# A new order of the first four blocks, other due times for later work, and 48 weight columns in the state sums of the second head

## The chip, the cores and the metric

The kernel runs on one core of a Trainium2 chip. Its engines work side by side, each in its own program order: TensorE (PE in the profile, with its weight loads apart as PEld), VectorE (DVE), ScalarE (ACT), GpSimd (POOL) and SyncE (SP). All transfers between DRAM and the core's memory are issued on SyncE's queue. The metric is the device time of one execution in microseconds (us), as the median of several runs; three runs of the kernel before gave 516.4 to 516.85 us, median 516.7 us.

## The reference

Attention with a decaying state, and behind it a feed-forward layer with a squared relu. B = 4 sequences, H = 8 heads, S = 768 steps, D = 48; 3072 tokens, 384 model columns, 2048 hidden columns.

```python
for t in range(S):
    state = alpha[:, :, t, :, None] * state + np.einsum('bhd,bhe->bhde', k[:, :, t], v[:, :, t])
    y[:, :, t] = np.einsum('bhd,bhde->bhe', q[:, :, t], state)
...
x = np.ascontiguousarray(attn_out.transpose(0, 2, 1, 3)).reshape(B * S, H * D)
h = np.maximum(x @ w_in, 0.0)
return (h * h @ w_out).astype(np.float32)
```

`w_in` and `w_out` arrive as 64-bit floats, which the kernel turns into 32-bit ones itself.

## The kernel before

**Blocks.** A block is 128 steps of one sequence, all heads: 24 blocks, numbered so that blocks 0 to 3 are the first 128 steps of the four sequences, 4 to 7 the next, and so on. Attention goes by blocks, two (a pair) at a time. The steps of a block n each have a short name, which the lists of the program use:

- `load`: q, k, v or alpha (a) of the block, 192 KB each, on SyncE's queue (L122)
- `ln`: logarithm of alpha (ACT, L267); `cs`: its running sum by a matmul with a triangle of ones (PE, L288, L291, L292)
- `eb`, `ei`: exp of the sums, and of their negative (ACT, L302, L305, L310)
- `mq`, `mk`: q and k scaled with these (DVE, L314)
- `qT`, `kT` and `qc`, `kc`: scaled q, k turned by four PE transposes each (L355) and copied out of PSUM (L371). From block 4 on `turn` does all of a pair's 32 transposes (T, L529) and ACT copies (L537)
- `sc`: scores inside each half of the block (PE, L418, bank `sckv`); `kv`: the block's contribution to the state, a sum over the steps of each half (PE, L441, the other part of that bank); `am`: masked scores (DVE, L426); `us`, `st`: state in the middle and at the end of the block (DVE, L452; L466, L467, the last one with the factors `last`)
- the last row of exp of the sums has to become a column, `last`. The first four blocks transpose it on PE (`lt`, L343) and copy it (`lc`, L349); later ones write it to DRAM (`bl`, L327) and read it back turned (`br`, L333, `last<-row`)
- `ya`, `yb`: the pair's output y (PE, L398), with a GpSimd nop between the two parts; `ga` and `gb` are the same with the scores, sums and state of the next pair ahead of them. `ea`, `ed`, `ev`: y copied into the transposed input x of the feed-forward (ACT and DVE, L562)

PSUM has eight banks, one pool (tag `att`) for everything.

**Feed-forward.** Four blocks, 512 tokens, make a group; there are six. Group 0 goes in plain f32: `ffn_in` (L926) computes a 128-column stripe j of the hidden layer, three matmuls, `ha` and `hb` are its two halves of 256 tokens, which a pair each makes ready; the output side (L760) follows. From group 1 on, weights and x are each split into a coarse part, a rest and a difference, and each product goes in three passes of a faster type (`h`, L681; `o`, L843, L855, L760). The parts of the weights are made on ACT and DVE by `prepare` (`cast_w`, `rest_w`, `diff_w`), those that don't fit are written to DRAM (`keep`) and streamed back for each group by `pump` (L644), as long as the number of tiles held is under `room`; the pool has 26 buffers.

**Weights.** Eight pieces of `w_in` and eight of `w_out`, 768 KB each. A piece is converted from 64 bits in three steps: `first` (DVE, two passes, L174 and L178), `middle` (ACT, L187 and L190), `second` (DVE, three passes, L196, L200, L203).

**What sets the order.** The first four blocks, the first three weight pieces and the first halves of group 0 stand in a list that is written out by hand (`first`, L980 to L989): each word calls a step, and every engine gets its instructions in the order of the words. `zeros2` there is three matmuls of a zero state tile with 256 columns (L384), `warm` one such (L244): fillers without a result. The words `gt`, `gs`, `gk`, `gy` hold the next load until an instruction of PE is done. Behind the list, `weave` (L1052) walks the units of the feed-forward, each with a cost, and puts in events (attention steps, weight conversions, splits) whose due time is reached. A pair's steps are due at the offsets of `PLAN` (L996) behind the pair's start, `EARLY` (L1011) for blocks under 8; the starts (`g0`, `g1`, `g`), the offsets of `ga` and `gb`, the spacing of the copies of y (`evs`), the start of the splits of x (`g1x`, `gx`), the pieces' preparation (`w_first`, `wstep`, `w_in_at`, `w_in_by`, `o0`, `o2`), the number of splits of the hidden layer put ahead (`lead`, `s0`, `ahead`) and `room` stand in the table `AT` (L19), all in units.

The state sums use 64 of k's columns as weights for both heads of a pair of heads: the first head writes partitions 0 to 63, the second 64 to 127 of the bank, of which 48 each are needed (the 16 between are zeros):

```python
out=ps[h][64 * e : 64 * (e + 1), 1, p, G:64],
lhsT=tile_of("k", n)[HALF[h], 2 * p + e, :],
```

Of the kernel before, what the change touches and what calls it, by code (L numbers as in the profile page):

```python
# [9 lines left out]
FP32 = mybir.dt.float32  # L10
# [5 lines left out]


GB = 4
AT = {'u0': 2, 'evs': 0.4, 'lead': 4, 'post': 3, 'w_first': (45.82, 44.44, 94.99), 'wstep': 2.31, 'w_in_at': 1.92, 'w_in_by': 3.02, 'room1': 25, 'room': 26, 's0': 3, 'ahead': 12, 'late': 23, 'xs': 0.35, 'g0': (-0.17, 20.59, 27.02), 'sc0': (2.36, 2.26, 2.42), 'g1': (7.68, 18.74, 27.21), 'g': (2.3, 15.42), 'g1x': 47.42, 'gx': 39.86, 'g0x': 55.51, 'k0': 2, 'h0': 16, 'k1': 5, 'h1': 0, 'h1by': 5, 'evs0': 0.23, 'tp': 'DDAD', 'tp1': 'AADD', 'split': 8, 'o0': (42.39, 46.35), 'o1': (), 'o2': (21.54, 19.65, 30.49, 26.1, 43.38, 50.96), 'str1': 14.0, 'ga': 9.32, 'gb': 12.97}  # L19


RUN = {0: 128, 32: 32, 64: 64, 96: 32}
# [3 lines left out]
def kernel(  # L26
# [12 lines left out]
    nc = tc.nc  # L39
    B, H, S, D = q.shape  # L40
    C = 128
    NCH = S // C
    NP = H // 2
# [4 lines left out]
    G = 64 - D  # L48
# [7 lines left out]
    ps_att = ctx.enter_context(tc.tile_pool(name="ps_att", bufs=8, space=PSUM))  # L56
# [11 lines left out]
    s_t = [s_all.pop(0) for _ in range(B)]  # L68
# [30 lines left out]
    def tile_of(x, n):  # L99
        return lent.get((x, n), tiles[x][n % len(tiles[x])])  # L100
# [142 lines left out]
    def warm(_):  # L243
        nc.tensor.matmul(  # L244
            out=ps_att.tile([128, NP, 64], FP32, tag="att", name="warm"),
            lhsT=s_t[0].rearrange("a p d -> a (p d)")[:, 0:128], rhs=s_t[0], start=True, stop=True,
        )

    for _ in range(3):
        warm(0)  # L250


    blk = [{} for _ in range(NBLK)]
# [16 lines left out]

    SPLIT = AT["split"]

# [135 lines left out]
    HALF = [slice(0, 64), slice(64, C)]  # L408
# [26 lines left out]
    def state_sums(n):  # L435
        ps = two[n]
        for p in range(NP):
            for e in range(2):
                first = (2 * p + e) * D
                for h in range(1 if n // B == NCH - 1 else 2):  # L440
                    marks["k", n] = nc.tensor.matmul(  # L441
                        out=ps[h][64 * e : 64 * (e + 1), 1, p, G:64],
                        lhsT=tile_of("k", n)[HALF[h], 2 * p + e, :],
                        rhs=tiles["v"][n % NV][HALF[h], first : first + D],
                        start=True, stop=True, skip_group_check=True,
                    )

    def sums_copied(n):

        ps = two.pop(n)  # L450
        u = blk[n]["u"] = u_all[n % 3]
        nc.vector.tensor_tensor(  # L452
            out=own(u), in0=own(ps[0][:, 1]), in1=own(s_t[n % B]), op=ALU.add
        )
        blk[n]["kv1"] = own(ps[1][:, 1])

    def own(x):
        return x[:, :, G:64]

    def next_state(n):  # L460
        blk[n]["s"] = s_t[n % B]
        if n // B < NCH - 1:
            s_all.append(s_t[n % B])
            s_t[n % B] = s_all.pop(0)
            s, last = own(s_t[n % B]), last_t[n % 4].unsqueeze(2).to_broadcast([128, NP, D])
            nc.vector.tensor_tensor(out=s, in0=blk[n].pop("kv1"), in1=own(blk[n]["u"]), op=ALU.add)  # L466
            nc.vector.tensor_tensor(out=s, in0=s, in1=last, op=ALU.mult)  # L467

# [118 lines left out]
    here, todo, room = {}, [], [22]  # L587
# [37 lines left out]
    def diff_w(w, p):  # L625
# [95 lines left out]
    def splits_of_x(at, g):  # L721
        return [(at + i * AT["xs"], f, (g, i % KM)) for i, f in enumerate((split_x,) * KM + (diff_x,) * KM)]

    def layer_in(g):
        units = []
        for n in range(NJ + 2):
            if n < NJ:
                units.append((1.05, in_x, (n,)))
            if 0 <= n - 2 < NJ:
                units.append((0.53, in_y, (n - 2,)))  # L730
            if 0 <= n - AT["post"] < NJ:
                units.append((0, in_post, (n - AT["post"],)))
            if AT["lead"] <= n < AT["lead"] + AHEAD and (g > 1 or AT["k1"] == NW):
# [240 lines left out]
    for x in "stky":  # L974
# [3 lines left out]
    steps["hb"] = lambda j: ffn_in(0, j, slice(HT, 2 * HT))  # L978
    steps["first"], steps["middle"], steps["second"] = convert_first, convert_middle, convert_second
    first = """  # L980
        zeros2 ln0 cs0 ln1 eb0 cs1 load0v ei0 mq0 mk0 load2a eb1 qT0 load3a qc0 mq1
        kT0 kc0 load1v ei1 qT1 mk1 load2k load2q qc1 sc0 kT1 weights0 kc1 kv0 load3q
        am0 lt1 sc1 ln2 us0 ln3 cs2 lt0 am1 load3k kv1 cs3 eb2 us1 ei2 gt1 mk2
        load2v weights1 ya0 mq2 yb0 lc1 gy0 eb3 kT2 lc0 load3v qT2 ei3 load4a zeros2
        st0 ea00 kc2 qc2 ed01 ed02 first0 zeros2 load4q mq3 zeros2 mk3 qT3 middle0
        qc3 kT3 second0 first1 kc3 lt3 lt2 sc2 kv2 am2 ea03 us2 sc3 kv3 gk3 middle1
        weights2 lc3 am3 us3 ha0 ya2 yb2 second1 weights3 ea20 lc2 ed21 ha1 ha3
        weights4 ed22 ed23 first2 st2 middle2 ha2 hb0 load4v hb1 st3 st1 load4k
    """  # L989
    for word in first.split():  # L990
        f = max((x for x in steps if word.startswith(x)), key=len)
# [2 lines left out]


    PLAN = (  # L996
        (-1.2, "ln0 ln1"),
        (-0.5, "sp0"),
        (0.0, "sp1"),
        (2.5, "cs0 cs1 eb0 ei0"),  # L1000
        (3.0, "eb1 ei1"),
        (3.5, "mk0"),
        (4.0, "bl0"),
        (4.5, "mq0 mk1 bl1"),
        (5.0, "mq1"),
        (6.5, "turn br1"),
        (7.0, "kc0 qc0 kc1 qc1 br0"),
        (9.5, "ga"),
        (10.5, "gb"),
    )  # L1010
    EARLY = (  # L1011
# [91 lines left out]
    for g in range(1, NG):  # L1103
        events = []
        if g + 1 < NG:
            n = GB * (g + 1) + 2
# [4 lines left out]
        if g == 1:  # L1111
# [5 lines left out]
            n = min(AT["k0"], AT["k1"])  # L1117
# [41 lines left out]
```

## Time and profile before

| | us |
|---|---|
| median of 3 runs | 516.7 |
| profiled execution, span from the first to the last instruction | 514.6 |
| TensorE busy | 508.3 |
| VectorE busy | 377.0 |
| ScalarE busy | 302.3 |
| GpSimd busy | 6.0 |

The page of the profile gives busy times by engine, and a line of the span in 40 slices, each digit the busy share (or the granted TensorE clock, PEclk) in tenths. The chain of waits is followed back from the last instruction; its pieces carry a start, a duration and the work. Rows of the timeline have a start, a duration, engine, line, operation, output and input with shapes, a count, and in brackets the idle time before and what ended it. Rows of grouped instructions have count, busy time, mean in ns, and idle time with its releaser. Rows of the stretches carry the busy time of each engine with its count of instructions, then the granted clock, the share of the DMA engines and GB/s. Rows of the waits: who waited for whom, the sum, how often, the longest. A matmul in f32 leaves two records.

The span begins with loads (the first logarithm starts at 3.68 us, the second at 6.90 us); blocks 0 and 1 have their y at 16 to 18 us, blocks 2 and 3 at 28 to 30 us; group 0's input side runs to 76.9 us, its output side to 124.5 us, group 1 to 212.3 us, and the last matmul ends at 511 us.

### The profile page before, as it was taken

What the parts mean: (1) busy time and instruction counts of PE and PEld (TensorE: products, weight loads), DVE (VectorE), ACT (ScalarE), POOL (GpSimd) and SP (SyncE); (2) the same over time, 40 slices, a digit from 0 to 9 for tenths busy, and PEclk for the clock granted to TensorE, in tenths of its full rate; (3) what the DMA queues carried; (4) which work ended last, traced back from release to release, by engine and by line L of the source; (5) the groups of instructions that cost most, each with busy time, mean ns of one, the idle gap of its engine ahead of it and who ended that gap; (6) DMA issues with size and microseconds to landing.
All of it is one profiled execution on the core that took longest, in us unless ns stands there. A gap on an engine that the chain in (4) does not pass through costs nothing.

```text
span 514.6 us, 12773 instructions
## 1 busy us (share of the span) xinstructions
PE 508.3 (99%) x5166; PEld 404.6 (79%) x5166; DVE 377.0 (73%) x656; ACT 302.3 (59%) x627; POOL 6.0 (1%) x33
## 2 busy tenths in 40 slices
PE   8999999999999999999999999999999999999997
PEld 6884456669877679988888888888888888888996
DVE  3798899898789869886698286799275588274961
ACT  4789875677788576376764175855075663144520
POOL 4000000000000000000000000000000000000000
PEclk9999999999999999999999999999999999999999
DMA  9989867272797788799975678894775544789201
GB/s 171 226 238 269 233 177 226 33 224 101 267 238 199 189 188 234 263 330 222 241 187 154 209 220 229 222 225 146 227 221 168 186 128 151 214 277 401 88 0 63
DMA packets 144794, 102.73 MB, mean 200 GB/s; under 512 B 116560, under 2 KB 118240, under 8 KB 144736
## 3 DMA queue, kind: packets, MB, share of 16 engines
q1 hardware_dynamic: 144736, 101.92, 70.4%
q8 instruction: 41, 0.67, 0.6%
q14 instruction: 17, 0.14, 0.1%
HBM read 84.57 MB, written 17.33 MB: 198 GB/s over the span
## 4 chain that ended last, share of the span: by engine, by line
PE 96%; DMA 2%; SPq 1%; DVE 1%; issue 0%; ACT 0%; DVEq 0%; POOLq 0%
PE h L681 31%; PE o L760 22%; PE o L843 13%; PE h L931 8%; PE o L855 6%; PE y L398 4%; PE sckv L418 3%; PE T L529 2%; PE sckv L441 2%; PE cs L288 1%; DMA a_in<-in_alpha_dram 1%; PE zeros L384 1%; DMA last<-row 1%; PE cs L291 1%; SPq L333 1%; PE cs L292 1%
## 5 line engine op out<-in xcount | busy, mean ns | idle before, releaser
L696 ACT ACTIVATE hid<-h 128x512 f32<-128x512 f32 x56 | 33.7, 601 | 88.4 <-PE h L681 86.7
L681 PE MATMUL h<-xd,wd 128*128 128x512 f32 x240 | 68.4, 398 | 0.0
L681 PE MATMUL h<-xa,wb 128*128 128x512 f32 x240 | 67.8, 391 | 0.0
L681 PE MATMUL h<-xl,wl 128*128 128x512 f32 x240 | 67.6, 390 | 0.0
L594 DVE TENSOR_TENSOR hid<-h,hid 128x512 f32<-128x512 f32 x56 | 38.5, 689 | 33.9 <-PE h L681 33.6
L562 ACT COPY x<-y 32x256 f32<-32x256 f32 (+1 forms) x137 | 48.9, 365 | 8.7 <-PE y L398 6.4
L681 PEld LDWEIGHTS h<-xl,wl 128*128 128x128 f32 x240 | 45.0, 188 | 9.6
L681 PEld LDWEIGHTS h<-xa,wb 128*128 128x128 f32 x240 | 44.9, 188 | 9.4
L681 PEld LDWEIGHTS h<-xd,wd 128*128 128x128 f32 x240 | 43.7, 188 | 9.2
L760 PE MATMUL o<-w_out,hid 128*128 128x384 f32 x144 | 48.9, 492 | 0.0
L931 PE MATMUL h<-x,w_in 128*128 128x512 f32 (+1 forms) x120 | 43.0, 511 | 0.0
L655 ACT ACTIVATE ha<-hid 128x512 fp32r<-128x512 f32 x42 | 26.7, 638 | 26.1 <-DVE hx L656 12.8
L760 PEld LDWEIGHTS o<-w_out,hid 128*128 128x128 f32 x144 | 26.7, 190 | 17.2
L710 DVE SCALAR_TENSOR_TENSOR hid<-hid 128x512 f32<-128x512 f32 x56 | 37.8, 684 | 0.0
L931 PEld LDWEIGHTS h<-x,w_in 128*128 128x128 f32 x120 | 22.4, 190 | 16.9 <-issue 13.9
L855 PE MATMUL o<-hd,wd 128*128 128x512 f32 x144 | 33.4, 391 | 0.0
L656 DVE SCALAR_TENSOR_TENSOR hl<-ha,hid 128x512 fp32r<-128x512 f32 x42 | 28.8, 686 | 4.7 <-ACT ha L655 4.4
L855 PEld LDWEIGHTS o<-hd,wd 128*128 128x128 f32 x144 | 26.8, 188 | 6.1 <-ACT o L848 0.6
L594 DVE TENSOR_TENSOR hd<-ha,hl 128x512 fp32r<-128x512 f32 x42 | 29.1, 692 | 1.9
L843 PE MATMUL o<-hx,wb 128*128 128x512 f32 x72 | 28.4, 394 | 0.0
L843 PE MATMUL o<-hx,wl 128*128 128x512 f32 x72 | 28.0, 389 | 0.0
L843 PE MATMUL o<-ha,wb 128*128 128x512 f32 x72 | 28.0, 389 | 0.0
(130 smaller groups left out, 950.4 us busy)
## 6 DMA issues: line engine op xcount, KB each, us to landing
wd<-do SPq DMA_DIRECT2D x37, 384.0 KB
wl<-lo SPq DMA_DIRECT2D x34, 384.0 KB
wl<-li SPq DMA_DIRECT2D x32, 384.0 KB
wd<-di SPq DMA_DIRECT2D x32, 384.0 KB
raw<-in_moe_w_in_dram SPq DMA_DIRECT2D x8, 768.0 KB
raw<-in_moe_w_out_dram SPq DMA_DIRECT2D x8, 768.0 KB
v_in<-in_v_dram SPq DMA_DIRECT2D x24, 192.0 KB
a_in<-in_alpha_dram SPq DMA_DIRECT2D x22, 192.0 KB
```

Source lines behind the costliest of these rows:

```text
L398: ins = nc.tensor.matmul(out=ys[e][64 * half : 64 * half + D + G * e, m % 2, p // 2, t], lhsT=lhsT, rhs=rhs, start=(half, e) not in seen, ...
L562: copy(out=x[kk][to : to + m, t : t + 2], in_=blk[n]["y"][e][r : r + m, :, p // 2],)
L594: nc.vector.tensor_tensor(out=o, in0=x, in1=z, op=op)
L655: nc.scalar.activation(out=a, in_=x, func=AF.Copy, scale=NEAR * E)
L656: nc.vector.scalar_tensor_tensor(out=l, in0=a.bitcast(FP32), scalar=-1.0 / E, in1=x, op0=ALU.mult, op1=ALU.add)
L681: nc.tensor.matmul(out=acc["h", j], lhsT=here[w, "i", p][:, kk, jj * 128 : (jj + 1) * 128], rhs=x_parts[x][:, kk], start=start and kk == 0 ...
L696: nc.scalar.activation(out=hid[j], in_=x, func=AF.Copy, scale=E)
L710: nc.vector.scalar_tensor_tensor(out=h, in0=h, scalar=0.0, in1=h, op0=ALU.max, op1=ALU.mult)
L760: nc.tensor.matmul(out=acc[t][:, 0:DM], lhsT=lhs[:, t * C : (t + 1) * C], rhs=rhs, start=start, stop=stop, skip_group_check=True,)
L843: nc.tensor.matmul(out=acc[c], lhsT=by_parts(here[w, "o", p], jj, c), rhs=x, start=n == 0 and w == "b", stop=n == NJ - 1 and w == "l", ski ...
L855: nc.tensor.matmul(out=acc[c], lhsT=by_parts(here["d", "o", p], n % 2, c), rhs=h_diff[n], start=False, stop=last and n == NJ - 1, skip_gro ...
L931: nc.tensor.matmul(out=ps, lhsT=w[:, kk, c0 : c0 + 128], rhs=xT[g][kk][:, cols], start=(kk == 0), stop=(kk == KM - 1),)
```

## The change

The list of the first four blocks is reordered. The first weight load goes ahead of v of block 1, `first0` ahead of the first masks, `middle0` ahead of the scaling of k of block 2; the fillers become seven `warm` (three ahead of the list as before) and three `zeros2` (before: three and four); the weight pieces, the copies of y and the half stripes `ha`, `hb` change places. `PLAN` and `AT` get other numbers, among them `g` from (2.3, 15.42) to (2.59, 16.44), `ga` from 9.32 to 9.22, `gb` from 12.97 to 13.41, `g1` from (7.68, 18.74, 27.21) to (9.3, 18.13, 28.01), `g1x` from 47.42 to 51.0, `gx` from 39.86 to 41.05, `lead` from 4 to 5, `s0` from 3 to 4, `ahead` from 12 to 10, `room1` (group 1) from 25 to 23, `room` from 26 to 27, `str1` from 14.0 to 2.65, `w_first` from (45.82, 44.44, 94.99) to (40.13, 41.4, 99.74), `o0` from (42.39, 46.35) to (41.66, 48.39). A new tile `pad` is taken from the PSUM pool behind the first three fillers, with no matmul in it (`pad` is 0). The second head's state sums take 48 weight columns, write partitions 64 to 111, and the VectorE steps on the state cover 112 partitions.

```diff
+    ps = ps_att.tile([128, NP, 64], FP32, tag="att", name="pad")
+    for _ in range(AT["pad"]):
+        nc.tensor.matmul(
...
-                first = (2 * p + e) * D
+                first, wide = (2 * p + e) * D, D if e else 64
...
-                        out=ps[h][64 * e : 64 * (e + 1), 1, p, G:64],
-                        lhsT=tile_of("k", n)[HALF[h], 2 * p + e, :],
+                        out=ps[h][64 * e : 64 * e + wide, 1, p, G:64],
+                        lhsT=tile_of("k", n)[HALF[h], 2 * p + e, 0:wide],
...
     def own(x):
-        return x[:, :, G:64]
+        return x[0 : 64 + D, :, G:64]
...
     first = """
-        zeros2 ln0 cs0 ln1 eb0 cs1 load0v ei0 mq0 mk0 load2a eb1 qT0 load3a qc0 mq1
-        kT0 kc0 load1v ei1 qT1 mk1 load2k load2q qc1 sc0 kT1 weights0 kc1 kv0 load3q
-        am0 lt1 sc1 ln2 us0 ln3 cs2 lt0 am1 load3k kv1 cs3 eb2 us1 ei2 gt1 mk2
-        load2v weights1 ya0 mq2 yb0 lc1 gy0 eb3 kT2 lc0 load3v qT2 ei3 load4a zeros2
-        st0 ea00 kc2 qc2 ed01 ed02 first0 zeros2 load4q mq3 zeros2 mk3 qT3 middle0
-        qc3 kT3 second0 first1 kc3 lt3 lt2 sc2 kv2 am2 ea03 us2 sc3 kv3 gk3 middle1
-        weights2 lc3 am3 us3 ha0 ya2 yb2 second1 weights3 ea20 lc2 ed21 ha1 ha3
-        weights4 ed22 ed23 first2 st2 middle2 ha2 hb0 load4v hb1 st3 st1 load4k
+        zeros2 warm0 ln0 cs0 ln1 load0v cs1 eb0 load2a eb1 ei0 mq0 mk0 lt1 qT0 mq1 kT0 ei1
+        kc0 qT1 warm0 ln2 cs2 mk1 load3a kT1 weights0 qc0 load1v qc1 first0 kc1 eb2 sc0 ln3
+        kv0 ei2 load2k lt0 sc1 kv1 warm0 am0 warm0 cs3 load2q load3q us0 load3k weights1
+        lc0 load2v am1 us1 middle0 mk2 eb3 ya0 yb0 load3v kT2 gy0 lc1 mq2 mq3 qT2 ei3 ea00
+        st0 gt1 zeros2 mk3 qT3 qc2 zeros2 ed02 kT3 ed01 kc2 qc3 first1 load4q load4a kc3
+        lt3 sc2 kv2 sc3 lt2 kv3 ea03 second0 am2 middle1 am3 ha0 us2 us3 lc2 ya2 load4k yb2
+        lc3 gk3 weights3 ea20 second1 ed22 ed21 first2 weights4 ha1 weights2 load4v ed23
+        middle2 ha3 ha2 st1 st2 hb1 st3 hb0
     """
...
     PLAN = (
-        (-1.2, "ln0 ln1"),
-        (-0.5, "sp0"),
-        (0.0, "sp1"),
-        (2.5, "cs0 cs1 eb0 ei0"),
-        (3.0, "eb1 ei1"),
-        (3.5, "mk0"),
-        (4.0, "bl0"),
-        (4.5, "mq0 mk1 bl1"),
-        (5.0, "mq1"),
-        (6.5, "turn br1"),
+        (-0.93, "ln0 ln1"),
+        (-0.63, "sp0"),
+        (-0.51, "sp1"),
+        (2.25, "cs0 cs1 eb0 ei0"),
+        (2.73, "eb1 ei1"),
+        (3.14, "mk0"),
+        (4.49, "bl0"),
+        (4.57, "mq0 mk1 bl1"),
+        (5.02, "mq1"),
+        (6.99, "turn br1"),
         (7.0, "kc0 qc0 kc1 qc1 br0"),
-        (9.5, "ga"),
+        (9.64, "ga"),
         (10.5, "gb"),
     )
```

More of the change, by code (lines that the diff above doesn't have):

```diff
@@ L18 @@
 GB = 4
-AT = {'u0': 2, 'evs': 0.4, 'lead': 4, 'post': 3, 'w_first': (45.82, 44.44, 94.99), 'wstep': 2.31, 'w_in_at': 1.92, 'w_in_by': 3.02, 'room1': 25, 'room': 26, 's0': 3, 'ahead': 12, 'late': 23, 'xs': 0.35, 'g0': (-0.17, 20.59, 27.02), 'sc0': (2.36, 2.26, 2.42), 'g1': (7.68, 18.74, 27.21), 'g': (2.3, 15.42), 'g1x': 47.42, 'gx': 39.86, 'g0x': 55.51, 'k0': 2, 'h0': 16, 'k1': 5, 'h1': 0, 'h1by': 5, 'evs0': 0.23, 'tp': 'DDAD', 'tp1': 'AADD', 'split': 8, 'o0': (42.39, 46.35), 'o1': (), 'o2': (21.54, 19.65, 30.49, 26.1, 43.38, 50.96), 'str1': 14.0, 'ga': 9.32, 'gb': 12.97}
+AT = {'pad': 0, 'u0': 2, 'evs': 0.21, 'lead': 5, 'post': 3, 'w_first': (40.13, 41.4, 99.74), 'wstep': 2.47, 'w_in_at': 2.02, 'w_in_by': 2.52, 'room1': 23, 'room': 27, 's0': 4, 'ahead': 10, 'late': 23, 'xs': 0.26, 'g0': (-0.17, 20.59, 27.17), 'sc0': (2.3, 2.23, 2.45), 'g1': (9.3, 18.13, 28.01), 'g': (2.59, 16.44), 'g1x': 51.0, 'gx': 41.05, 'g0x': 55.56, 'k0': 2, 'h0': 18, 'k1': 5, 'h1': 0, 'h1by': 5, 'evs0': 0.42, 'tp': 'DDAD', 'tp1': 'AADD', 'split': 8, 'o0': (41.66, 48.39), 'o1': (), 'o2': (21.47, 19.65, 32.98, 28.08, 41.44, 51.99), 'str1': 2.65, 'ga': 9.22, 'gb': 13.41}
 RUN = {0: 128, 32: 32, 64: 64, 96: 32}
@@ L250 @@
         warm(0)
+    ps = ps_att.tile([128, NP, 64], FP32, tag="att", name="pad")
+    for _ in range(AT["pad"]):
+        nc.tensor.matmul(
+            out=ps[:, 0, 0:8], lhsT=s_t[0].rearrange("a p d -> a (p d)")[:, 0:128],
+            rhs=s_t[0][:, 0, 0:8], start=True, stop=True,
+        )
     blk = [{} for _ in range(NBLK)]
@@ L464, in next_state @@
             s_t[n % B] = s_all.pop(0)
-            s, last = own(s_t[n % B]), last_t[n % 4].unsqueeze(2).to_broadcast([128, NP, D])
+            s, last = own(s_t[n % B]), last_t[n % 4][0 : 64 + D].unsqueeze(2).to_broadcast([64 + D, NP, D])
             nc.vector.tensor_tensor(out=s, in0=blk[n].pop("kv1"), in1=own(blk[n]["u"]), op=ALU.add)
```

## The prediction

> **What bounds the kernel now.** I read the page's busy times first, then TensorE's own waits, then the chain of work that ended last, piece by piece, and only then the first 30 us engine by engine.
>
> ```profile
> span 514.6 us, 12773 instructions
> PE 508.3 (99%) x5166; PEld 404.6 (79%) x5166; DVE 377.0 (73%) x656; ACT 302.3 (59%) x627; POOL 6.0 (1%) x33
> PEclk9999999999999999999999999999999999999999
> ```
>
> TensorE is busy in all but 6.3 us, at the granted clock throughout, so apart from its own work only gaps and fillers can move the time. Behind the first 2 us its matmuls show two waits of 0.2 us or more for another engine's result (a third, for a copy of k, is as short as the second):
>
> ```profile
> PE cs L288 <- ACT a_in L267: 0.5, 1, 0.5
> PE sckv L418 <- DVE hid L594: 0.2, 1, 0.2
> ```
>
> The chain (start, duration, work) shows the front. A matmul of f32 leaves two records, so x18 is nine fillers of zeros.
>
> ```profile
> 11.73 0.61 PE sckv L441 x32
> 15.99 1.12 PE y L398 x62
> 18.49 0.44 PE qT L355 x4
> 18.92 3.89 PE zeros L384 x18
> 27.80 1.42 PE y L398 x60
> 29.31 0.69 PE y L398 x31
> 30.00 12.04 PE h L931 x48
> 67.86 0.62 PE sckv L418 x32
> 68.48 0.45 PE sckv L441 x32
> 510.99 0.36 DVE osb L594
> ```
>
> The order of work from 30.00 us on has the same matmuls in both kernels, and the tail after 510.99 us (3.6 us to the span's end) is untouched. What decides is when y of blocks 2 and 3 ends (30.00 us now), and the gaps behind it. The same 32 records of state sums take 0.61 us at 11.73 and 0.45 us at 68.48: until about 18.4 us TensorE goes at three quarters of its later pace, though the granted clock reads 9.
>
> Behind 30 us these pieces are longer than their like:
>
> ```profile
> 143.69 0.90 PE T L529 x24
> 144.60 0.46 PE T L529 x8
> 162.91 1.15 PE T L529 x32
> 169.21 0.95 PE y L398 x60
> 170.30 0.79 PE y L398 x31
> 181.48 0.77 PE T L529 x16
> 182.25 0.71 PE T L529 x16
> 188.11 1.41 PE y L398 x92
> 238.14 0.28 PE L418 MATMUL sckv<-qs,ks 48*64 48x64 f32 x2
> 239.80 4.31 PE h L681 x18
> ```
>
> Thirty-two transposes (T) take 1.15 us where nothing is late; the two slow sets take 1.36 and 1.48, so 0.21 + 0.33 = 0.54 us is lost. Scores and sums at 238.14 last until 239.80, 1.66 us; at 67.86 they take 0.62 + 0.45 = 1.07: 0.59 lost. The y at 169.21 lasts until 171.09, 1.88 us, against 1.41: 0.47 lost. That is 1.6 us, all that the later part can give back by better timing.
>
> **The change part by part: the front.** The first weight load moves ahead of v of block 1 and of k, q of blocks 2 and 3 in SyncE's queue, and its first two VectorE passes (first0) now stand before the masks (am0) instead of behind y of blocks 0 and 1. One filler is added ahead of the first sums of logs, one behind qT1, two behind kv1; the nine zeros become six.
>
> ```profile
> 6.00:10.75 4.75, 3.92 (x37) 2.20 (x39) 2.72 (x5) 3.19 (x7) 0.90 (x5) 1.00 1.27 195
> 13.90:16.60 2.70, 2.70 (x85) 1.86 (x88) 1.59 (x6) 1.45 (x4) 0.00 (x0) 1.00 1.00 296
> 6.90 0.52 ACT L267 ACTIVATE a_in<-a_in 128x384 f32<-128x384 f32 x1 [2.70 <-DMA a_in<-in_alpha_dram]
> 11.59 0.82 SPq L122 DMA_DIRECT2D raw<-in_moe_w_in_dram  x1
> 12.45 0.79 DVE L426 COPY_PREDICATED am<-halves_mask,sckv 128x256 f32<-128x256 uint32 x2 [1.68 <-issue]
> 15.26 0.36 DVE L452 TENSOR_TENSOR us<-sckv,s 128x192 f32<-128x192 f32 x1 [1.11 <-PE sckv L441]
> 18.74 1.33 DVE L562 COPY x<-y 64x256 f32<-64x256 f32 x3 [1.39 <-ACT x L562]
> 20.00 0.54 DVE L174 TENSOR_SCALAR power<-raw 128x768 uint32<-128x768 uint32 x1
> 22.23 0.96 DVE L196 SCALAR_TENSOR_TENSOR power<-raw,power 128x768 uint32<-128x768 uint32 x1 [0.28 <-ACT power L187]
> 27.69 0.35 DVE L452 TENSOR_TENSOR us<-sckv,s 128x192 f32<-128x192 f32 x1
> ```
>
> (The first two rows are stretches; their last column is GB/s.) When do the weights land? Nine small loads of 0.197 MB stand ahead of them; with 195 GB/s they are through at about 10.75 us. The weights, 0.79 MB, moved at 296 GB/s in the stretch that they filled: 2.7 us, so 13.4. The logarithm of the second alpha started at 6.90, some 1.1 us after its bytes (the fourth load) were through; so the weights are usable at 14.5, and v of block 1, a load later, at about 15.1.
>
> VectorE is in order: first0 (2 x 0.54) ends at 15.6 and am0 starts there, not at 12.45. From am0's start to the end of the second us it had 3.17 us with 1.11 idle: 2.1, with one copy of the last row (0.2) more, so both us are done at 17.9. Queued behind first0 are am0, us0, am1, us1, and TensorE's y waits for them. TensorE by then has kv1 (v at 15.1, scores ready; 0.6 us at the slow pace, to 16.0), two fillers (0.43 each by the zeros' row, 0.57 at three quarters) and a sum of logs (384 columns to the filler's 256, so 0.86), so 18.0: the two sides meet, and y starts 2.0 us later than the 15.99 of now. Y's two parts take 1.9 us as now (1.12, a nop, 0.69 as at 29.31; 15.99 to 17.90), to 19.9.
>
> From there to the second y TensorE had 27.80 - 17.90 = 9.9 us of unbroken work; three zeros less (3 x 0.43 = 1.3) leave 8.6, so 28.5. VectorE needs less: from 15.62 (15.26 + 0.36) to 28.04 (27.69 + 0.35, the last us) it had 12.4 us with 1.39 and 0.28 idle; without first0, which is behind it, 9.7, so 27.6. The second y then starts at 28.5 without the 0.2 us that it waited inside 1.42, and ends at about 30.4 instead of 30.00. The front costs **+0.4 us**. The filler ahead of the sums of logs delays cs0 by 0.4 to 0.8 us; cs0 is used only after the second logarithm (to 7.42), so nearly all of it is hidden, and the rest is inside the wait for the weights. If weights landed a microsecond sooner VectorE gains it, but TensorE's row of fillers doesn't; if later, all of it shows. Both ends: -1.2 (rival one) and +3.3 (rival two).
>
> **The 48 weight columns.** 176 of the 352 matmuls of the state sums get narrower weights; their moving columns stay 48.
>
> ```profile
> 102.84 0.62 PE y L398 x31
> ```
>
> With 64 moving columns the scores (all weights 64 wide) and y (half its weights 48 wide) take the same 0.62; the sums with 64 weight columns but 48 moving take 0.45. The moving side sets the pace, so I take nothing. If weights set it, half the loads a quarter shorter saves an eighth of 22 sets of 0.45 us: 1.2 us, the other end; a loss has no row for it, since y runs with that mixture. VectorE's 112 instead of 128 partitions change no element count along a row: nothing.
>
> The Trainium skill ("TensorE: Matmul & The Clock Gate", "LDWEIGHTS (loading the stationary operand)") says that a weight load lasts in proportion to its columns; by that alone the sums would gain, and the rows above speak against it.
>
> **The later part.** Turn moves from 6.5 to 6.99 units behind a pair's start while the scalings ahead of it stay within 0.07: 0.47 units more, and a unit here is about 1.3 us (six h matmuls at 4.31 / 18 = 0.24 us count 1.05 units), so 0.6 us, more than either loss. The 0.54 goes. Turn also gets nearer to the scores at ga, 2.23 units (2.9 us) instead of 2.82:
>
> ```profile
> 182.61 0.64 ACT L537 COPY ks<-T 128x256 f32<-128x256 f32 x2
> L656 DVE SCALAR_TENSOR_TENSOR hl<-ha,hid 128x512 fp32r<-128x512 f32 x42 | 28.8, 686 | 4.7 <-ACT ha L655 4.4
> ```
>
> The 1.15 of T and four copies at 0.32 make 2.4 us, so the scores aren't late unless ACT has a queue; its loads of q, issued with turn, are used a pair later. gb moves 0.44 units behind, ga 0.10 forward; by the order of instructions gb falls one step of three matmuls (0.7 us) later behind ga, which would cover the 0.59. But that loss came through a wait for the last row:
>
> ```profile
> 233.06 3.86 DMA last<-row
> DVE s L467 <- DMA last<-row: 10.0, 3, 4.2
> ```
>
> VectorE stood until 237, with the hid evictions queued behind it, and TensorE waited for those banks. The last row's transfer is issued behind streamed tiles in SyncE's queue, and with room 27 for 26 buffers each streamed tile is issued one release earlier than its buffer is free, so it can block the queue. I count half of the 0.59: -0.3. The wait of y at 169 has no named cause: 0, with -0.47 as its other end. The x splits at 51.0 instead of 47.42 leave 2.5 units, 3.3 us, to the end of group 1; three splits on VectorE (3 x 0.686, the row of hl) fit, the differences are due two steps later: nothing, or their excess, some 1 us, if VectorE is behind. Lead, s0, ahead, w_first, o0, o2 and str1 only move ACT and VectorE work that TensorE's gapless row hides now; room 23 makes fewer tiles prefetched before group 2. These I set at nothing.
>
> Sum against the profiled execution: 514.6 + 0.4 - 0.54 - 0.3 = 514.2 of span. The runs' median, 516.7, is 2.1 above that span, so 516.3.
>
> **The rivals.** *One, the front gets shorter.* If the slow pace ends by 10 us because TensorE is kept busier, and the weights are usable at 13.4, kv1 ends at 15.1 + 0.45, fillers and sum of logs (0.86 + 0.65) at 17.0, y at 18.6 (three quarters of 1.9, and the nop), the 8.6, of which some 0.2 was slow, at 27.0, and the second y at 28.9 instead of 30.00: 514.6 - 1.1 - 0.8 + 2.1 = 514.8. For it: the pace changed only after eight gapless microseconds, and fillers now stand where gaps were; against: the new order has idle stretches of its own before kT1. [...]
>
> *Two, the weights block VectorE (slower).* If the queue serves the weights mixed with the loads behind them, they end when those do: in the trace all bytes up to q of block 2 were through at 16.6, plus 1.1 makes 17.6. Then both us end at 21.0, and 1.9 + 8.6 + 1.9 later it is 33.4: +3.4 - 0.84, so 519.3. It decides once the weights come later than 14.6; against it, a small load's start followed its own bytes by 1.1 us.
>
> *Three, the queue blocks (slower).* One streamed tile more ahead of the last row, a release apart (nine h matmuls, 2.15 us), less the 0.7 of a later gb, is 1.45 us at each of three places where VectorE waits (10.0 us in all); at two of them 2.9, without the 0.3: 514.6 + 0.4 - 0.54 + 2.9 + 2.1 = 519.5. For it the 0.59 already lost; against, a wait of 4.2 us elsewhere cost TensorE nothing.
>
> *Four, the narrow weights pay:* 516.3 - 1.2 = 515.1.
>
> **How the numbers follow.** 0.2% is 1.03 us, about what a measurement of this kernel can tell from no change. The forecast has 0.45 (0.39 of it within the bound, 0.03 on either side), rival one 0.22, two 0.13, three 0.13 (0.04 of it small enough to stay within), four 0.07. Faster 0.32, same 0.43, slower 0.25. The forecast's own range is 515.4 to 517.3; to leave out no more than 2 in 10 it must reach to rival one's 514.8 and four's 515.1 and most of the way to 519.3: 514.5 to 518.8.
>
> **What would show it.** In the profile after: first0 (power, L174) starting at 14.5 with an idle time ended by a DMA (rival two: 17.6); the first y at 18.0 and the first gapless h stretch at 30.4; T of 32 records at 1.15 us everywhere in group 1; state sums still 0.45 us (rival four: below 0.42); VectorE's wait for the last row still about 10 us in all (rival three: 14). I am wrong if a wait of over 1 us by TensorE stands behind 31 us.

## The result, and the profile after

| | before | after |
|---|---|---|
| median, us (15 runs each) | 516.71 (515.88 to 518.08) | 518.02 (516.69 to 521.92) |
| span of the profiled execution, us | 514.6 | 517.4 |
| that execution, us | 516.7 (2.1 above its span) | 519.49 |

The changed kernel is slower: ratio 1.0031, 95% interval 1.0017 to 1.0044. That lies inside the predicted range, but not where the forecast put it ("about the same", 516.3). The profiled execution of after is 1.5 us above its median; its runs also spread wider, 5.2 us against 2.2.

The page of after, its two lines that answer to those of before:

```profile
span 517.4 us, 12766 instructions
PE 507.7 (98%) x5168; PEld 403.7 (78%) x5168; DVE 376.9 (73%) x656; ACT 301.9 (58%) x627; POOL 6.0 (1%) x33
```

TensorE is busy for 0.6 us less in a span that is 2.8 us longer: what was added is waiting. The waits of TensorE of 0.5 us or more (us in total, how often, the longest), without the filler's at the start:

```profile
PE h L937 <- DVE w_in L203: 1.2, 1, 1.2
PE cs L294 <- ACT a_in L273: 0.8, 1, 0.8
PE cs L349 <- ACT b_wide L308: 0.7, 1, 0.7
PE cs L297 <- DVE hi L285: 0.6, 1, 0.6
PE o L766 <- DVE osb L805: 0.6, 1, 0.6
PE h L687 <- DVE hid L600: 0.5, 1, 0.5
```

The second and third lie in the first 10 us, where the chain goes through the loads; the second stood in before with 0.5 us. None of the other four stood in the list of before. Where the time went, from the chain for the first row and the timelines for the starts of the others:

| | before | after | later by |
|---|---|---|---|
| second y ends | 30.00 | 31.82 | 1.8 |
| first `h` of group 1 | 124.36 | 125.71 | 1.4 |
| first `h` of group 2 | 212.12 | 215.07 | 3.0 |
| first `h` of group 3 | 291.54 | 294.35 | 2.8 |
| end of span | 514.6 | 517.4 | 2.8 |

So in these two executions 1.8 us are lost in the front, 0.5 are won in group 0, 1.6 lost in group 1, and little changes behind it. The medians differ by 1.3 us only: after's profiled execution shows more loss than its typical run has. *The front*, timeline rows of VectorE and TensorE (in brackets the idle time before and what ended it):

```profile
14.12 0.56 DVE L174 TENSOR_SCALAR power<-raw 128x768 uint32<-128x768 uint32 x1 [2.28 <-DMA raw<-in_moe_w_in_dram]
...
17.47 0.69 PE L404 MATMUL y<-qs,us 48*48 48x64 f32 x32
...
24.10 0.56 DVE L174 TENSOR_SCALAR power<-raw 128x768 uint32<-128x768 uint32 x1 [1.94 <-DMA raw<-in_moe_w_in_dram]
...
26.90 0.96 DVE L203 TENSOR_TENSOR w_in<-w_in,power 128x768 f32<-128x768 f32 x1
28.00 1.53 PE L937 MATMUL h<-x,w_in 128*128 128x256 f32 x6 [1.19 <-DVE w_in L203]
```

and the chain of waits (start, duration, work):

```profile
17.08 7.00 DMA raw<-in_moe_w_in_dram
...
28.00 1.55 PE h L937 x6
...
31.82 11.84 PE h L937 x48
```

The first weights are usable at 14.12 and the first y starts at 17.47. But at 24.10 there is a second wait for weights: `first1` is the first step on the *second* piece, whose load is issued at 17.08 and takes 7.00 us. `second0` needs only the first piece, yet stands behind `first1` on VectorE; so the weights for `ha0` are ready only at 27.9 and TensorE stands for 1.19 us. In the old list `second0` was ahead of `first1`.

*Group 1*, VectorE and TensorE in after:

```profile
171.78 0.36 DVE L472 TENSOR_TENSOR s<-sckv,us 112x192 f32<-112x192 f32 x1
174.43 0.36 DVE L473 TENSOR_TENSOR s<-s,last 112x192 f32<-112x192 f32 x1 [2.29 <-DMA last<-row]
174.71 0.35 DVE L285 CAST hi<-a_in 128x384 fp32r<-128x384 f32 x1
...
175.21 0.41 PE L297 MATMUL cs<-hi,causal_r 128*128 128x384 f32 x1 [0.62 <-DVE hi L285]
...
175.96 0.56 DVE L286 TENSOR_TENSOR lo<-a_in,hi 128x384 fp32r<-128x384 f32 x1
...
176.85 2.74 PE L766 MATMUL o<-w_out,hid 128*128 128x384 f32 x8
...
193.00 0.36 DVE L473 TENSOR_TENSOR s<-s,last 112x192 f32<-112x192 f32 x1 [1.26 <-DMA last<-row]
...
206.52 0.96 DVE L635 SCALAR_TENSOR_TENSOR wd<-wb,wl 128x768 fp32r<-128x768 f32 x1
207.40 1.94 DVE L805 SCALAR_TENSOR_TENSOR osb<-o,osb 128x384 f32<-128x384 f32 x4
208.00 7.23 PE L766 MATMUL o<-wd,hd 128*128 128x384 f32 x40 [0.58 <-DVE osb L805]
```

and the same steps in before:

```profile
169.10 0.36 DVE L279 CAST hi<-a_in 128x384 fp32r<-128x384 f32 x1
...
170.83 0.77 DVE L426 COPY_PREDICATED am<-halves_mask,sckv 128x256 f32<-128x256 uint32 x2
...
204.34 1.95 DVE L799 SCALAR_TENSOR_TENSOR osb<-o,osb 128x384 f32<-128x384 f32 x4
...
207.41 0.95 DVE L629 SCALAR_TENSOR_TENSOR wd<-wb,wl 128x768 fp32r<-128x768 f32 x1
```

In before, the split of the logarithms (`hi`, `lo`) is done ahead of the masks (`am`), and so long ahead of the state step `s` that waits for the last row. In after it stands behind that step: it inherits the 2.29 us, and the four sums of logs go at the pace of VectorE's splits (175.21 to 176.85, 1.64 us with 0.62 idle ahead, against 1.00 us, 173.41 to 174.41, in before). The eviction `osb` now stands behind a rest of weights (`wd`); that order alone costs TensorE nothing, as the last part of the experiments shows. It takes the 1.26 us at 193.00, in which VectorE stands for a last row once more, to make the wait of 0.58.

*Group 2*, the issues on SyncE, after and then before:

```profile
229.54 3.29 SPq L654 DMA_DIRECT2D wd<-di  x1
232.92 0.59 SPq L333 DMA_DIRECT2D row<-b  x2
```

```profile
225.25 1.40 SPq L327 DMA_DIRECT2D row<-b  x2
226.74 1.69 SPq L648 DMA_DIRECT2D wl<-li  x1
```

With `bl0` due at 4.49 instead of 4.0 units, the write of the rows comes behind a streamed tile that blocks the queue for 3.29 us, and goes out 7.7 us later, 4.7 of them if both are counted from the group's first `h`. In this execution it costs TensorE 0.5 us.

### The profile page after: what moved, and what is told of

It reads as the page before. It is cut to its first block, busy times and chain, and to the rows that moved or that the text cites. A ratio compares the mean times of both kernels' runs of the same rounds, so it can differ in the third digit from the quotient of the medians.

```text
span 517.4 us, 12766 instructions
## 1 busy us (share of the span) xinstructions
PE 507.7 (98%) x5168; PEld 403.7 (78%) x5168; DVE 376.9 (73%) x656; ACT 301.9 (58%) x627; POOL 6.0 (1%) x33
## 3 DMA queue, kind: packets, MB, share of 16 engines
HBM read 84.57 MB, written 17.33 MB: 197 GB/s over the span
## 4 chain that ended last, share of the span: by engine, by line
PE 86%; SPq 5%; DMA 3%; DVE 3%; ACT 2%; issue 1%; DVEq 0%; POOLq 0%
PE h L687 30%; PE o L766 19%; PE o L849 13%; PE h L937 8%; PE o L861 6%; PE y L404 4%; SPq L122 3%; PE T L535 2%; PE sckv L424 2%; DMA raw<-in_moe_w_in_dram 1%; PE sckv L447 1%; SPq L339 1%; DMA last<-row 1%; ACT x L568 1%; PE cs L298 1%
## 5 line engine op out<-in xcount | busy, mean ns | idle before, releaser
L687 PE MATMUL h<-xd,wd 128*128 128x512 f32 x240 | 66.9, 394 | 0.0
L568 ACT COPY x<-y 32x256 f32<-32x256 f32 (+2 forms) x137 | 48.3, 366 | 12.4 <-PE y L404 9.9
L849 PE MATMUL o<-hl,wl 128*128 128x512 f32 x72 | 28.0, 390 | 0.0
```

Of the source, the lines that this page charges most:

```text
L568: copy(out=x[kk][to : to + m, t : t + 2], in_=blk[n]["y"][e][r : r + m, :, p // 2],)
L687: nc.tensor.matmul(out=acc["h", j], lhsT=here[w, "i", p][:, kk, jj * 128 : (jj + 1) * 128], rhs=x_parts[x][:, kk], start=start and kk == 0 ...
L849: nc.tensor.matmul(out=acc[c], lhsT=by_parts(here[w, "o", p], jj, c), rhs=x, start=n == 0 and w == "b", stop=n == NJ - 1 and w == "l", ski ...
```

## The experiments

The kernels take the change apart or mend steps of it. Those below were timed in five rounds, each against before on the same chip (four batches on three chips, so kernels of different batches are compared by their ratios); y (end of the second y) and the lengths of groups 1 and 2 (from a group's first `h` to the next one's) are in us, from each one's single profiled execution. The ratios are of medians over 5 (h_room), 6 (f_piece) or 10 to 15 executions.

| kernel | ratio (interval) | highest run | y | group 1 | group 2 |
|---|---|---|---|---|---|
| before | 1 | 517.25 to 520.39 by batch | 30.00 | 87.8 | 79.4 |
| after | 1.0031 (1.0017, 1.0044) | 521.92 | 31.82 | 89.4 | 79.3 |
| a_list | 1.0015 (1.0004, 1.0025) | 518.39 | 31.24 | 87.3 | 78.9 |
| b_numbers | 1.0014 (1.0002, 1.0026) | 519.12 | 30.05 | 88.8 | 78.8 |
| c_columns | 1.0000 (0.9988, 1.0012) | 517.46 | 29.79 | 87.5 | 78.8 |
| d_first1 | 1.0019 (1.0004, 1.0035) | 519.81 | 30.16 | 88.5 | 78.8 |
| e_split | 1.0022 (1.0005, 1.0039) | 519.24 | 30.83 | 88.4 | 79.0 |
| f_piece | 1.0081 (1.0056, 1.0105) | 522.79 | 31.14 | 88.5 | **82.2** |
| g_all | 1.0034 (1.0015, 1.0053) | 521.10 | 32.10 | 87.0 | **82.5** |
| h_room | 1.0032 (1.0019, 1.0045) | 518.75 | 31.03 | 88.4 | 78.8 |
| i_row | 1.0006 (0.9996, 1.0017) | 518.03 | 30.15 | 88.6 | 78.8 |
| j_list | 1.0006 (0.9997, 1.0015) | 517.45 | 30.71 | 87.3 | 78.8 |
| k_piecerow | 1.0034 (1.0017, 1.0052) | 520.64 | 30.59 | 88.4 | 78.8 |
| l_four | 1.0002 (0.9989, 1.0014) | 518.96 | 31.13 | 88.5 | 79.0 |
| m_oldlist | 0.9999 (0.9984, 1.0014) | 519.77 | 30.13 | 87.0 | 79.4 |
| n_oldlist_row | 1.0019 (1.0003, 1.0034) | 520.60 | 29.84 | 89.4 | 78.8 |

**The three parts alone.** Before with the new list, with the new tables, with the narrow columns:

```diff
-        zeros2 ln0 cs0 ln1 eb0 cs1 load0v ei0 mq0 mk0 load2a eb1 qT0 load3a qc0 mq1
...
+        zeros2 warm0 ln0 cs0 ln1 load0v cs1 eb0 load2a eb1 ei0 mq0 mk0 lt1 qT0 mq1 kT0 ei1
...
```

> The kernel before with the new list of the first four blocks alone (its fillers among it; no pad tile, old numbers, 64 columns). Theory, front: the second weight piece lands late (24.1 us in the profile after), first1 waits for it in VectorE's order with second0 queued behind, and y of blocks 2 and 3 ends at 31.8 instead of 30.0; then this run is 1.3 to 1.9 us slower than before (ratio 1.0025 to 1.0037), and the end of the second y stands at 31.5 to 32 us. Rival, later part: the numbers cause the loss; then this run is within 0.5 us of before.

```diff
-AT = {'u0': 2, 'evs': 0.4, 'lead': 4, ...
+AT = {'pad': 0, 'u0': 2, 'evs': 0.21, 'lead': 5, ...
-        (4.0, "bl0"),
+        (4.49, "bl0"),
...
```

> The kernel before with the new numbers (due times, offsets, room) alone. Theory, front: the later part is nearly even, -0.5 to +0.5 us, as its gains (transposes no longer late, 0.5 us) and its losses (the split of the logarithms behind a wait for the last row, an eviction behind a weight piece) cancel. Rival, later part: +1.1 us or more (in the two profiles the time from the second y to the end grew by 1.0 us).

```diff
-                first = (2 * p + e) * D
+                first, wide = (2 * p + e) * D, D if e else 64
...
```

> The kernel before with 48 weight columns in the second head's sums alone. Both theories: no change, within 0.2 us; 32 records of state sums still in 0.45 us. A weight-bound sum would be 1.2 us faster.

List and tables cost about 0.8 and 0.7 us, the columns nothing: the parts add up to 1.0029, after measured 1.0031. The list cost less than expected (1.0015 for at least 1.0025), the tables' 0.7 us fell between the two expectations. The sums of the state confirm that the columns give nothing; in after's timeline 32 of them with the narrow weights start 0.45 us ahead of what follows, as in before:

```profile
69.92 0.62 PE L447 MATMUL sckv<-v_in,k_in 64*64 64x48 f32 x32
70.37 0.68 PE L424 MATMUL sckv<-qs,ks 48*64 48x64 f32 x32
```

**The front: `first1` behind `second0`**, in after and in before with the new list.

```diff
-        ... qc2 qc3 first1 load4q load4a kc3
+        ... qc2 qc3 load4q load4a kc3
-        lt3 sc2 kv2 sc3 lt2 kv3 ea03 second0 am2 middle1
+        lt3 sc2 kv2 sc3 lt2 kv3 ea03 second0 first1 am2 middle1
```

> The changed kernel with first1 behind second0 in the list (one word moved), so that VectorE converts the first weights while the second piece is still on its way. Theory, front: the wait of TensorE for the first weights (1.2 us) goes, the second y ends at 30.2 to 30.5 us, and the run is 1.2 to 1.6 us faster than the changed kernel (about 516.5). Rival, later part: the second y gets earlier, but the time stays within 0.5 us of the changed kernel, or first1 waits just as long with the masks behind it (second y at 31.5 or later).

> The kernel before with the new list alone, and in it first1 behind second0. Theory (the list loses only by first1's wait for the second piece of weights): second y of the front ends at 30.1 us or sooner, TensorE has no wait for w_in of 0.5 us, ratio 0.9995 to 1.0005. Rival (the list's order of loads costs by itself): ratio 1.0010 or more, as the list with first1 in its place (1.0015).

Against their partners both fell, 1.0031 to 1.0019 and 1.0015 to 1.0006, but the intervals overlap, so it is not settled what the move is worth. Nor do the profiles settle it: TensorE's wait for `w_in` is gone in both, but after's is the only one of all profiles that has it. a_list has none, and neither have the other four with `first1` ahead of `second0`. The profiles of all kernels with the new list, those with `first1` moved on top:

| | first weights | wait for the second | second y ends |
|---|---|---|---|
| d_first1 | 13.74 | | 30.16 |
| i_row | 14.01 | | 30.15 |
| j_list | 14.55 | | 30.71 |
| l_four | 14.64 | | 31.13 |
| g_all | 14.59 | | 32.10 |
| k_piecerow | 13.97 | 0.85 | 30.59 |
| h_room | 14.34 | 0.97 | 31.03 |
| e_split | 14.55 | 0.99 | 30.83 |
| a_list | 14.38 | 1.23 | 31.24 |
| f_piece | 14.61 | 1.32 | 31.14 |
| after | 14.12 | 1.94 | 31.82 |

With `first1` moved, the second y ends 16.1 to 16.5 us after the first weights are usable; in g_all it is 17.5, with a gap of 0.93 us in TensorE's y that no record explains. With `first1` ahead of `second0` it is 16.3 to 16.9 us for waits up to 1.32 us, and 17.7 in after, where the second piece lands last. So this order costs TensorE a microsecond or more when that piece is late, and little otherwise. j_list fell between the two expectations (1.0006; its second y at 30.71 missed the 30.1 expected): its first weights landed at 14.55, and that time the new list hands on in full, while the old list's y ended between 29.79 and 30.13 us in all five profiles that have it.

**The split, the o2 piece, all three, the room.** After with one number each, and g_all with the first two and the moved `first1`:

```diff
-'g1': (9.3, 18.13, 28.01)
+'g1': (9.3, 18.13, 27.8)
```

> The changed kernel with the third pair of group 1 begun at 27.8 instead of 28.01, so that the split of its logarithms (hi, lo; due at 27.17 and 27.29) stands in VectorE's order ahead of ga of the pair before (27.35), whose state step waits for the last row, and not behind it. Theory (numbers: that wait, with the split queued behind it, holds up the sums of logs): TensorE's wait for hi (0.6 us) goes, the stretch from group 1's to group 2's first h matmul falls from 89.4 to about 88 us, and the time by 0.7 to 1.4 us against the changed kernel (ratio to before 1.0005 to 1.0018). Rival (the wait is covered or only moves): the stretch stays over 89 us and the ratio at 1.0025 or more.

```diff
-'o2': (21.47, 19.65, 32.98, 28.08, 41.44, 51.99)
+'o2': (21.47, 19.65, 32.98, 28.08, 43.38, 51.99)
```

> The changed kernel with the fifth of the w_out pieces prepared at 43.38 (as before) instead of 41.44 in group 1, so that its last step (0.95 us on VectorE) stands behind the evictions of the output sums, not ahead of them. Theory: TensorE's wait for the eviction (osb, 0.6 us) goes, and the time falls by 0.4 to 0.8 us (ratio 1.0015 to 1.0023). Rival: another step holds the evictions up as long, ratio unchanged near 1.003.

> The changed kernel with all three repairs (first1 behind second0, third pair at 27.8, fifth piece at 43.38). Theory: the three losses add, so 1.0031 less 0.0012, 0.0018 and 0.0011 gives a ratio of about 0.999 (516 us or a little under), with the second y ended by 30.2 and the stretch of group 1 at 87.5 us or less. Rival: they share one slack, and the ratio stays over 1.001.

```diff
-'room': 27
+'room': 26
```

> The changed kernel with room at 26 instead of 27. The prediction's rival three (a streamed tile placed one release early blocks SyncE's queue ahead of the last row): VectorE's wait for the last row falls from 10.7 us to 8 or less and the time by 0.6 us or more. Theory (the streamed tile starts at the same release either way): no change, within 0.4 us of the changed kernel (ratio 1.0023 to 1.004).

The earlier split takes the sums' wait away, as expected, but in its execution the wait for `osb` was 1.26 us, and its ratio, 1.0022, missed the expected 1.0005 to 1.0018. Room 26 did not change the time (1.0032 from five runs): that rival's cause is out. VectorE's wait for the last row did come down to 7.9 us, as the rival expected, but it was 7.9 in d_first1 with room 27 too. The later o2 piece, which should have mended the eviction, made the kernel clearly slower, and g_all gained nothing either. Both lost it in group 2. VectorE and TensorE in f_piece there:

```profile
241.43 0.36 DVE L473 TENSOR_TENSOR s<-s,last 112x192 f32<-112x192 f32 x1 [5.22 <-DMA last<-row]
...
243.05 1.65 PE L687 MATMUL h<-xa,wb 128*128 128x512 f32 x3 [1.85 <-DVE hid L600]
244.49 1.49 PE L687 MATMUL h<-xl,wl 128*128 128x512 f32 x3
...
247.44 0.85 PE L687 MATMUL h<-xl,wl 128*128 128x512 f32 x3
```

and its stretches of 1 us (busy time of PE, PEld, DVE, ACT, POOL with counts, the granted clock, DMA share, GB/s):

```profile
242.00:243.00 1.00, 0.00 (x0) 0.00 (x0) 1.00 (x3) 0.61 (x2) 0.00 (x0) 1.00 1.02 409
243.00:244.00 1.00, 0.95 (x2) 0.84 (x3) 0.96 (x3) 0.00 (x0) 0.00 (x0) 0.50 1.07 304
244.00:245.00 1.00, 1.00 (x4) 0.75 (x3) 0.97 (x3) 0.00 (x0) 0.00 (x0) 0.50 1.13 263
...
246.00:247.00 1.00, 1.00 (x5) 0.79 (x5) 0.93 (x4) 0.96 (x2) 0.00 (x0) 0.80 0.26 28
247.00:248.00 1.00, 1.00 (x6) 0.84 (x5) 1.00 (x3) 0.98 (x3) 0.00 (x0) 1.00 0.73 151
```

VectorE stands 5.22 us for the last row, the evictions of `hid` wait behind it, and TensorE stands for 1.85 us. Then the granted clock is 0.50 for 3.4 us: three matmuls take 1.65 and 1.49 us where three take 0.85 at 247.44. At half pace 3.4 us do the work of 1.7, so a wait of 1.85 us costs about 3.5; the stage is 3.4 us longer (82.2 against 78.8). g_all shows the same: 2.18 us of wait, then 0.50 for 3.2 us.

How long TensorE waits hangs on when `s` gets its last row. Counted from the first `h` of group 2, that step of VectorE began at 24.9 to 26.2 us in six of the profiles with the new numbers, none with a wait of TensorE for `hid`; in the other six (l_four, e_split, after, m_oldlist, f_piece, g_all) it began at 26.32, 26.35, 26.62, 26.77, 27.96 and 28.37 us, and TensorE waited 0.16, 0.23, 0.50, 0.59, 1.85 and 2.18 us. Why the later o2 piece makes the row so late is not shown.

**The rows ahead of the streamed tile.** Both writes of a pair's rows due at 4.0 units (in before the first was due at 4.0, the second at 4.5); with the moved `first1`, with f_piece's number, and with everything:

```diff
-        (4.49, "bl0"),
-        (4.57, "mq0 mk1 bl1"),
+        (4.0, "bl0 bl1"),
+        (4.57, "mq0 mk1"),
```

> d_first1 with both steps that write the last rows (bl0, bl1) due at 4.0 units instead of 4.49 and 4.57. In SyncE's order both rows of group 2's first pair then stand ahead of the streamed tile wd that took 3.28 us to issue there. Theory (the row's write stands behind that tile, VectorE stands for the last row, and in some executions TensorE with it): the row of that pair is issued at about 226 instead of 229.4 us, no execution comes over 518.7 us (d_first1 reached 519.81), ratio 1.0005 to 1.0013. Rival (the spread has another source): highest over 519, ratio 1.0019 or more.

> f_piece with both rows due at 4.0 units. In f_piece VectorE stood 5.22 us for the last row, TensorE 1.85 us for VectorE's hid, and behind that the granted clock was 0.50 for some 3 us (group 2 stage 82.2 us, ratio 1.0081). Theory (all of that hangs on the row's place in the queue): the row goes out some 3 us sooner, TensorE's wait is below 0.3 us, the clock stays at 1.00, the stage takes 79 us, ratio 1.0015 to 1.0035. Rival (the later piece of weights costs by itself): ratio 1.006 to 1.010.

> g_all (the repairs of first1, of the split at 27.8 and of o2's fifth piece) with both rows due at 4.0 units: the orders on TensorE and VectorE are those of g_all, only SyncE's differs. Theory: group 2 takes 79 us instead of 82.5, no half clock, no execution over 518.5 us, ratio 0.9990 to 1.0008. Rival (the wait in group 2 comes from the load on the DMA engines, not from the place in the queue): ratio 1.002 to 1.005, a highest of over 520 us.

l_four has the orders of g_all on TensorE and VectorE and another on SyncE alone. The rows' writes in g_all and in l_four, and then what came of it in l_four:

```profile
232.07 0.60 SPq L333 DMA_DIRECT2D row<-b  x2
```

```profile
228.58 2.19 SPq L333 DMA_DIRECT2D row<-b  x2
...
239.75 0.36 DVE L473 TENSOR_TENSOR s<-s,last 112x192 f32<-112x192 f32 x1 [3.57 <-DMA last<-row]
...
241.37 0.97 PE L687 MATMUL h<-xa,wb 128*128 128x512 f32 x3 [0.16 <-DVE hid L600]
```

The rows go out 3.5 us sooner (4.0 from the first `h`), VectorE stands 3.57 instead of 5.56 us, TensorE 0.16 instead of 2.18, and the clock stays whole. The medians follow: 1.0081 to 1.0034 and 1.0034 to 1.0002, intervals apart in both pairs; i_row against d_first1 (1.0019 to 1.0006) points the same way with intervals that overlap. So the place of the row in the queue is shown as the cause of what f_piece and g_all lost. For after itself it is not: k_piecerow, with the row's place and the later o2 piece, stays at 1.0034, no better than after, and after with the row's place alone was not run. It is not the only source of long runs either: k_piecerow still reached 520.64, and l_four, expected to stay under 518.5, 518.96. What is shown for after is that the four changes together take its loss away: l_four's interval ends at 1.0014, after's begins at 1.0017.

**The old list under the new numbers**, with all later repairs, and with the rows' alone:

```diff
-        zeros2 warm0 ln0 cs0 ln1 load0v cs1 eb0 load2a eb1 ei0 mq0 mk0 lt1 qT0 mq1 kT0 ei1
...
+        zeros2 ln0 cs0 ln1 eb0 cs1 load0v ei0 mq0 mk0 load2a eb1 qT0 load3a qc0 mq1
...
```

> l_four with the list of the kernel before. Theory (with first1 repaired the new list still ends its second y some 16.3 us after the first weights land, 30.2 to 31.1 us; the old list does not depend on that and ends at 30.0): second y at 30.0 in the profile, the later part as in l_four or better, median 0.3 to 0.6 us below l_four's ratio: 0.9985 to 0.9998. Rival (what is left is in the later numbers): ratio 1.0002 or more.

> The kernel after with the list of the kernel before and both rows due at 4.0 units, without the other two later repairs. Theory (the split of the logarithms behind the waiting state step costs 0.6 to 1.6 us in group 1, the eviction behind a rest of weights 0.6): ratio 0.0010 to 0.0025 above m_oldlist's. Rival (only the row's place mattered): within 0.0006 of m_oldlist.

The two differ by the split and the o2 piece only. n_oldlist_row has both waits of after, m_oldlist has neither, and their group 1 differs by 2.4 us (89.4 and 87.0). From n_oldlist_row:

```profile
172.47 0.36 DVE L473 TENSOR_TENSOR s<-s,last 112x192 f32<-112x192 f32 x1 [2.18 <-DMA last<-row]
173.24 0.41 PE L297 MATMUL cs<-hi,causal_r 128*128 128x384 f32 x1 [0.51 <-DVE hi L285]
...
206.25 7.20 PE L766 MATMUL o<-wd,hd 128*128 128x384 f32 x40 [0.77 <-DVE osb L805]
```

The ratios (1.0019 and 0.9999) differ as expected, though their intervals overlap. m_oldlist is the best version found, and not to be told from before: the new numbers, once mended, give nothing back that can be measured.

What the o2 piece does for `osb` shows only with all profiles of the new numbers side by side. TensorE waited for `osb` only where VectorE had stood for the last row some 14 us before, at 190 to 193 us. With `wd` ahead of `osb`, such waits of 1.26 (after), 1.45 (n_oldlist_row) and 1.96 us (e_split) were followed by waits of TensorE of 0.58, 0.77 and 1.26; b_numbers, d_first1, h_room and i_row, with the same order and no such wait, had none. With `osb` ahead of `wd`, 1.41, 1.62 and 1.65 us (f_piece, g_all, m_oldlist) had no consequence, and only l_four's 3.11 came through:

```profile
192.36 0.36 DVE L473 TENSOR_TENSOR s<-s,last 112x192 f32<-112x192 f32 x1 [3.11 <-DMA last<-row]
...
206.36 5.84 PE L766 MATMUL o<-wd,hd 128*128 128x384 f32 x32 [1.26 <-DVE osb L805]
```

So the wait comes from the last row here too; the place of the piece sets how much of it is covered, 0.7 or 1.85 us. This is also why l_four's group 1 took 88.5 us with everything mended.

## Why the prediction went wrong

*The bound, and the columns:* right. TensorE's work did not change, and the columns measured 1.0000 against a forecast of nothing; rival four is out.

*The first weights and the first y:* right. 14.12 and 17.47 were measured, 14.5 and 18.0 forecast. Rival one (the slow pace ends sooner) did not come; the first y came 0.5 us ahead of the sum, and the weights 0.4 ahead.

*The "three quarters" pace:* a misreading, which did not decide the forecast. It set sums of the state behind other matmuls (0.61 us) against sums behind scores (0.45). Like compared with like, the trace of before is as fast early as late; both of these sums of logs stand behind matmuls of the `sckv` bank:

```profile
13.33 0.84 PE cs L288 x2
...
72.79 0.84 PE cs L288 x2
```

Behind fillers or `h` the same pair takes 0.65, at 17.33 us in j_list as at 74.24 in after; and j_list has sums of the state at 0.45 behind scores (25.36) and at 0.61 behind a transpose (26.66). A filler behind fillers takes 0.43 us at 5.43 us in after, as the zeros of before do at 19. So what costs is a change from one shape of matmul to another, 0.15 to 0.2 us each time. Rival one had no slow pace to lose, and the sum of logs ahead of the first y took 0.65 us, not 0.86.

*"VectorE needs less: ... so 27.6":* this step failed. It let VectorE run on without waits from the first y to the last us and so never asked which piece `first1` reads. That piece's load was behind others in the queue, landed at 24.1 in the profile, and `second0` stood behind it, for 1.19 us of waiting on TensorE. How much of this a typical run has stays open, since no other profile shows that wait. The forecast for the rest of the step holds where `first1` is moved: y at 30.15 to 31.13, and 32.10 in g_all, 30.4 forecast. Rival two had the kind of mishap right (weights that block VectorE) and the wrong piece. The front was forecast at +0.4 us; the list alone measured +0.15%, 0.8 us. (The "both ends" of the front, -1.2 and +3.3, are -1.1 and +3.4 in the paragraphs on the rivals, whose sums use those.)

*The later part, -0.84:* the 0.54 of the transposes came, as the chain of after shows (the same sets took 1.36 and 1.48 us in before, at 143.69 and 181.48);

```profile
147.75 1.15 PE T L535 x32
...
185.20 1.14 PE T L535 x32
```

the other terms did not. "These I set at nothing" covered due times that change VectorE's order: the split of the logarithms moved behind a step that waits, and an eviction behind a rest of weights, which left it 0.7 us of cover for a late row. VectorE's order was costed by durations, which fit, and not by what each instruction waits for. For the last row the sum credited 0.3 to a later gb, and did not price `bl0` and `bl1` at all, though they were moved past a streamed tile on SyncE's queue. Forecast -0.84, measured +0.14% for the tables alone, 0.7 us.

*Rival three* named the right place (last row, queue, VectorE, hid) and the wrong cause: room 26 gave 1.0032. VectorE's wait for the last row came to 10.7 us in all in after, near the 10 forecast, so its sum gave no warning; what counts is when the one ahead of `hid` ends. Nor did the sign that the forecast named for being wrong appear, a wait of TensorE of over 1 us behind 31 us: the longest there was 0.62 us in after.

So the two terms were off by +0.4 and by +1.6 us; from 516.3 that gives 518.3, against the 518.02 measured. Each of the two rests on a ratio known to some 0.6 us, so the agreement is no proof of the shares.

## What to carry to other kernels

Before moving a step forward on an in-order engine, look up for every operand of the steps that pass each other when its transfer lands; durations that fit are not enough, since the step that waits hands its wait to all behind it. A short transfer that a chain hangs on (a row written and read back) belongs ahead of bulk tiles in the queue, and its due time is part of the cost of any retiming. A mended kernel should be read in several profiles: whether a wait of 0.5 us becomes one of 2 us differed from one kernel to the next although their orders were nearly the same.

## What was not expected of the hardware

A gap of 1.85 or 2.18 us on TensorE was followed by 3.2 to 3.4 us at a granted clock of 0.50; gaps of 1.26 us (e_split, l_four), 1.19 us (front of after) and 0.59 us (m_oldlist) were not, the clock read 1.00 there. So in these profiles a wait costs its own length up to somewhere between 1.26 and 1.85 us, and behind that about 1.7 us more. The Trainium skill ("TensorE: Matmul & The Clock Gate", "What's actually happening") has the clock fall to half after an idle window of some 3.4 us and come back after as long a stretch of work. The half and the length of the slow stretch agree; the gap that sets it off was shorter here. Such stretches also fit the longest runs. One of 3.4 us lowers the mean granted clock of an execution of 519 us by 0.003, and the two profiled ones read 0.997. On record are eleven executions of over 520 us, and all read 0.995 to 0.998 (521.92 of after 0.995, one of before with 520.39 us 0.997). Where in those executions the clock fell, and behind which wait, is not shown. Runs of 519 to 520 us with 0.999 or 1.00 (519.73 in after) must have another reason.
